# Three of four sine classes computed on ScalarE, products re-ordered and small transfers queued behind x's first tile, in a Fourier mixing + squared-ReLU kernel

## The chip, the cores and the metric

The kernel runs on one core of a Trainium2 chip. The metric is device time in microseconds (us) of one execution of the whole program. The times of the runs before the change lie between 1917.63 and 1918.9 us.

## The reference

```python
x        # (8, 3008, 256) float32
w_in     # (256, 2048), scaled by a float64 number, so float64
w_out    # (2048, 256), float64 in the same way

X = np.fft.fft(x, axis=1)            # along the sequence
X = np.fft.fft(X, axis=2).real       # along the features; keep the real part
h = X.reshape(24064, 256) @ w_in
g = np.maximum(h, 0) ** 2
out = (g @ w_out).astype(np.float32)
```

## The kernel before

**The mathematics.** The transform along the sequence is a product with cosine and sine tables. Rows of `x` are first folded: sums and differences of the rows n, S-n, M-n and M+n (S = 3008, M = S/2) halve the work several times, so that only S/4+1 row groups are left. The feature transform is folded into `w_in`: instead of transforming the features, the kernel multiplies `w_in` by a 256x128 cosine matrix (`cosd`, giving `G1`) and a sine matrix (`sind`, giving `G2`). The folded rows times cosine give `Pt`, times sine give `Qt`; both are 128 features by 1505 frequencies. A middle feature column is kept apart and handled by products called "E".

**The row tiles.** The row groups are cut into seven tiles, numbered 0 to 6. Tile 0 (95 rows) is the first class, tile 1 (94 rows) the second, tiles 2 and 3 (96 and 92 rows, `TWO` and `TWO + 1`) the third, and tiles 4, 5 and 6 (128, 128 and 120 rows, `ODD0` to `NT - 1`) the fourth. A product of a tile with its table has 95, 189 or 377 columns for each of two parities (`kp`). The tables `cosT` and `sinT` lie in SBUF, each tile's columns beside the next's. `load_table` fetches a tile's part in one to three transfers, since the rows that a tile needs are scattered in the array in device memory.

**Names for the steps.** In the hand-written order, "Pt" for a number t (P0, P1, ...) is the cosine product of tile t, "Qt" (Q0, Q1, ...) its sine product, and "Et" (E0, E1, ...) the cosine product of the lone middle column. Each is two matmuls on TensorE, one for each parity. `folds_of("P0")` is VectorE's work before the product P0, `folds_of("Q0")` that before Q0. `win[0][1]()` multiplies the first piece of `w_in` by `cosd` and `sind` (line 315) and copies the results to `G1` and `G2` on ScalarE (line 316). `p_part("copy")` is a pair of ScalarE copies of partial results (line 650, into `da`). The joins `join_4`, `join_2` and `lo` (lines 667 to 679, through `both`) combine the partial results on VectorE; `lo` writes `Pt` or `Qt`. `f_e` (line 518) is a tiny ScalarE operation that puts a tile's lone column into `lone` (shown as `wsum` in the profile) and must come before that tile's E product. `rounded` and `begin_win` change a piece of float64 weights into float32: VectorE lines 274, 276, 291, 293, 300, ScalarE lines 280, 281, 283.

**The order.** Nothing is re-ordered by a scheduler (`manual_schedule`): each engine executes its instructions in the order in which the program emits them, and a waiting instruction holds everything behind it on its engine. The code after `start()` (line 1062) is the first phase, the transform of batch element 0, which nothing precedes. It ends with `Qt` (line 667), the small product at line 828, and the first product of the main loop (lines 858 and 859). The main loop then runs over 8 batch elements x 6 frequency blocks x 8 pairs of feed-forward chunks; each step makes h (`front`), squares its positive part on ScalarE (`combine`) and multiplies by `w_out` (`back`). The transform of the next batch element is woven into it.

**The queues of the first phase.** SyncE (the SP queue) issues, in this order: x tiles 0 and 1, the first piece of `w_in` (two transfers), x tiles 2 and 3, `cosd`, `sind`, x tiles 4, 5, 6, cosine tables of tiles 4, 5, 6, sine tables of tiles 4, 5, 6, the next pieces of `w_in`. GpSimd (the POOL queue) issues: six transfers of the cosine tables of tiles 0 and 1, one of `alt_d` (a column of +1 and -1 that becomes the last column of `sind`), four of the cosine tables of tiles 2 and 3, ten of the sine tables of tiles 0 to 3. Each queue uses eight completion semaphores in turn: a transfer is issued only when the one eight places before it has landed.

**Keeping TensorE warm.** `awake(48)` at the start issues 48 products that nobody reads (tile `filled`, line 228); `awake(10)` does so again before the main loop.

Of the kernel before, what the change touches and what calls it, by code (L numbers as in the profile page):

```python
# [8 lines left out]
F32 = mybir.dt.float32  # L9
# [4 lines left out]
P = 128  # L14
# [23 lines left out]
def row_tiles(S):  # L38

    q = S // 4  # L40
    tiles, at = [], 0
    for count in (q // 2 + 1, q // 2):
        assert 2 * P < count <= 3 * P
        for r in range(0, count, P):
            tiles.append((at + r, min(P, count - r)))
        at += count
    return tiles


def class_tiles(S):  # L50


    half = S // 8 + 1
    tiles = []
    for c, order in enumerate((range(0, half, 4), range(2, half, 4), range(1, half, 2), range(half, S // 4 + 1))):
        size = -(-len(order) // -(-len(order) // P) // R) * R
        for r in range(0, len(order), size):
            tiles.append((c, order[r], order.step, len(order[r:r + size])))
    return tiles


def column_counts(S):

    counts = []
    for kp in range(2):
        n0 = len(range(kp, S // 4 + 1, 2))
        n1 = (n0 + 1) // 2
        n2 = (n1 + 1) // 2
        counts.append((n2, n2, n1, n0))
    return counts  # L70


def table_places(S):

    places, at = [], 0
    for c, *_ in class_tiles(S):
        places.append(at)
        at += column_counts(S)[0][c]
    return places, at
# [3 lines left out]
def kernel(  # L83
# [12 lines left out]
    nc = tc.nc  # L96
# [8 lines left out]
    CH = 256  # L105
    CK = 251
    NX = 3
    TILES = class_tiles(S)
    NT = len(TILES)
    NC = column_counts(S)  # L110
    PLACE, WT = table_places(S)
# [14 lines left out]
    psh = ctx.enter_context(tc.tile_pool(name="psh", bufs=2, space=PSUM))  # L126
    psd = ctx.enter_context(tc.tile_pool(name="psd", bufs=2, space=PSUM))
    psm = ctx.enter_context(tc.tile_pool(name="psm", bufs=1, space=PSUM))
# [5 lines left out]
    xt = {}  # L134
# [3 lines left out]
    ODD0 = NT - 3  # L138
# [15 lines left out]
    def later_rows(t):  # L154

        if t >= ODD0:
            return [(p, S // 8 + 1 + first, count, 1) for p, first, count in ODD[t - ODD0]]
        c, r0, step, rows = TILES[t]
        if t == TWO + 1:
            return [(p, TILES[TWO][1] + step * (2 * HALF2 - p - R), R, step) for p in range(0, ROWS2, R)]  # L160
        return [(0, r0, rows, step)]

    def load_x(b, t):
        if b and (t >= ODD0 or t == TWO + 1):
            xt[b, t] = xp.tile([P, 4, D], F32, name="xt", tag="x")
            for p, first, count, step in later_rows(t):
                nc.sync.dma_start(out=xt[b, t][p:p + count], in_=x[b, first:first + step * (count - 1) + 1:step])
            return
        c, r0, step, rows = TILES[t]

        while rows % 15 and rows % 16 and r0 + step * rows < NROW:
            rows += 1

        pool, tag = (gp, "g") if b == 0 and t < NT - NX else (xp, "x")
        xt[b, t] = pool.tile([P, 4, D], F32, name="xt", tag=tag)
        nc.sync.dma_start(out=xt[b, t][0:rows], in_=x[b, r0:r0 + step * (rows - 1) + 1:step])
# [8 lines left out]
    sind = const.tile([P, 2, P], F32, name="sind")  # L185
    cosT = const.tile([P, 2, WT], F32, name="cosT")
    sinT = const.tile([P, 2, WT], F32, name="sinT")
# [7 lines left out]
    def load_table(tab, src, tiles, queue=nc.sync):  # L195

        for t in tiles:
            c, r0, step, rows = TILES[t]
            for i, (s0, count) in enumerate(row_tiles(S)):
                mine = [r for r in range(count) if (s0 + r - r0) % step == 0 and 0 <= (s0 + r - r0) // step < rows]  # L200
                if mine:
                    o, m = (s0 + mine[0] - r0) // step, len(mine)
                    while m % 15 and m % 16 and o + m < P and mine[0] + step * m < P:
                        m += 1
                    nk = NC[0][c]
                    queue.dma_start(out=tab[o:o + m, :, PLACE[t]:PLACE[t] + nk],
                                    in_=src[mine[0]:mine[0] + step * (m - 1) + 1:step, :, i, 0:nk])

    make_identity(nc, ident)
    last = ident[:, P - 1:]  # L210

# [13 lines left out]
    def awake(n):  # L225
        filled = psh.tile([P, CH], F32, name="filled", tag="h")
        for _ in range(n):
            nc.tensor.matmul(filled[:, 0:P], ident, ident, start=True, stop=True)


    def pair_in(j):

        return moe_w_in.rearrange("(c p) (h j f) -> j c p h f", p=P, j=NJ, h=2)[j]
# [5 lines left out]
    def parts(w, k):  # L239
        return w.rearrange("p c (e h) -> p h (c e)", h=k)  # L240
# [10 lines left out]
    def load(src):  # L251

        nonlocal raws
        pool, tag = (gp, "g") if raws in (1, 2) else (xp, "x") if raws % (NX + 1) else (ep, "c")
        raws += 1
        single = src.dtype == F32
        raw = pool.tile([P, 2, CH, 1 if single else 2], src.dtype if single else U32, name="raw", tag=tag)
        for c in range(2):
            nc.sync.dma_start(out=raw[:, c].rearrange("p (o e) w -> p o (e w)", o=src.shape[2]),
                              in_=src[c] if single else src[c].bitcast(U32))  # L260
        return raw
# [44 lines left out]
    def begin_win(j, shared=False):  # L306

        w = ep.tile([P, 2, CH], F32, name="win", tag="sB" if j % 2 else "sA")
        finish = convert(parts(w, 1), win.pop(j, None) or load(pair_in(j)), shared)

        def products():
            for tab, G, nm in ((cosd, G1, "mC"), (sind, G2, "mD")):
                pg = psm.tile([P, CH], F32, name="pg", tag=nm)
                for i in range(2):
                    nc.tensor.matmul(pg, tab[:, i], w[:, i], start=i == 0, stop=i == 1)  # L315
                nc.scalar.copy(G.rearrange("p (h j f) -> j p h f", h=2, j=NJ)[j],
                               pg.rearrange("p (h f) -> p h f", h=2))

        def for_e():

            ps = psd.tile([P, CH], F32, name="pe", tag="d")
            for h in range(2):
                fc = j + NJ * h
                nc.tensor.matmul(ps[:, h:h + 1], G2[:, fc * P:(fc + 1) * P], last, start=True, stop=True)

            return lambda: nc.vector.tensor_scalar_mul(gE[:, j::NJ], ps[:, 0:2], 0.5)

        win[j] = finish, products, for_e
# [24 lines left out]
    turn = const.tile([P, 3, 4], F32, name="turn")  # L353
# [684 lines left out]
    def p_part(*names):  # L1038
        for nm in names:
            for kp in range(2):  # L1040
                groups[0, kp, nm]()
# [6 lines left out]
    def rounded(j):  # L1048
        halves, product, _ = win[j][0]
        halves()  # L1050
        product()


    def folds_of(names):
        for nm in names.split():
            (for_p if nm[0] == "P" else for_q)(int(nm[1:]))

    def products_of(names):
        for nm in names.split():
            (p_part if nm[0] == "P" else q_part)({"P": "", "Q": "", "E": "e"}[nm[0]] + nm[1:])  # L1060

    start()
    awake(48)
    load_x(0, 0)
    load_x(0, 1)
    nc.scalar.copy(turn[0:1, 0, 0:1], ident[0:1, 0:1])
    load_table(cosT, cos_s, (0, 1), nc.gpsimd)
    folds_of("P0 Q0 P1 Q1")
    begin_win(0)
# [2 lines left out]
    for dst, src, queue in ((cosd, cos_d, nc.sync), (sind[:, :, 0:P - 1], sin_d, nc.sync), (sind[:, :, P - 1:], alt_d, nc.gpsimd)):  # L1072
        queue.dma_start(out=dst, in_=src.rearrange("(c p) m -> p c m", p=P))
    load_table(cosT, cos_s, (TWO, TWO + 1), nc.gpsimd)
    for t in range(ODD0, NT):
        load_x(0, t)
    load_table(cosT, cos_s, range(ODD0, NT))
    load_table(sinT, sin_s, range(ODD0), nc.gpsimd)
    load_table(sinT, sin_s, range(ODD0, NT))
    win[1] = load(pair_in(1))  # L1080
    win[2] = load(pair_in(2))
    folds_of("P2")
    rounded(0)
    products_of("P0 P1")
    win[0][1]()
    products_of("E0 E1")
    folds_of("P3")
    products_of("P2 P3")
    p_part("copy")
    products_of("E2 E3")  # L1090
    folds_of("P4 P5 Q2 P6 Q3 Q4")
    products_of("P4 P5 P6 E4 E5 E6 Q0 Q1 Q2 Q3")
    for nm in ("join_4", "join_2", "lo"):
        groups[0, 0, nm]()
    folds_of("Q5")
# [101 lines left out]
    for i in range(len(steps) + LAG + 4):  # L1197
        if i < len(steps):
            b, k0, n, j = steps[i]
# [22 lines left out]
        if i >= LAG and flight:  # L1222
            at, g_, s_ = flight.pop(0)
# [75 lines left out]
```

## Time and profile before

| What | Value |
|---|---|
| Median of 3 runs | 1918.27 us (1917.63 to 1918.9) |
| The profiled execution: its time | 1918.66 us |
| The profiled execution: its span | 1916.9 us, with 1.8 us around it |
| TensorE (PE) busy, share of the span | 1906.6 us, 99% |
| VectorE (DVE) busy | 1443.3 us, 75% |
| ScalarE (ACT) busy | 954.7 us, 50% |
| GpSimd (POOL) busy | 1135.0 us, 59% |
| Granted TensorE clock, mean | 0.999 |
| Moved by DMA | 69.58 MB; of it 10.48 MB in the first 50 us |

The busy shares are averages over the whole span. The change touches only the first 40 us, where they are different, so this part has to be read from views that are cut by time: the busy time by stretches, the timeline, the waits, and the landing of transfers. In the timeline a line gives the start, the time from the first to the last of a group, the engine, the line of the kernel, what is written and read, how many, and in brackets how long the engine was idle before it and what ended that. A float32 product on TensorE shows as two records, so a count of 8 is four matmuls.

### The profile page before, as it was taken

The numbers are of one execution on the slowest core, as the hardware profiler recorded it, in microseconds if no ns is written. First come the engines' busy times: TensorE is split into PE (matmuls) and PEld (weight loads), VectorE is DVE, ScalarE is ACT, GpSimd is POOL, SyncE is SP. The second block draws the span as 40 slices with busy tenths as digits, with TensorE's granted clock in tenths as the row PEclk, the third lists the DMA queues.
The fourth block names the chain that finished last, engine by engine and source line by source line (L and its number), as shares of the span: only waits on it lengthen the run. The fifth ranks groups of instructions, "written<-read, shape, count | busy, mean of one in ns | idle before, by whom it ended". The sixth has DMA issues, their size and how long they took to land.

```text
span 1916.9 us, 28146 instructions
## 1 busy us (share of the span) xinstructions
PE 1906.6 (99%) x9250; PEld 1698.0 (89%) x9250; DVE 1443.3 (75%) x3645; ACT 954.7 (50%) x1207; POOL 1135.0 (59%) x1731
## 2 busy tenths in 40 slices
PE   9999999999999999999999999999999999999998
PEld 7888898888988898888988889888898888988887
DVE  8998887787678876787768877788767777655554
ACT  3755554555454544455444454455544555444444
POOL 3265655665566555655566665566655665566565
PEclk9999999999999999999999999999999999999999
DMA  8341211110111101111011100111001101100100
GB/s 219 116 46 28 56 28 37 28 45 13 28 36 42 34 12 36 33 42 28 12 36 47 36 20 12 47 39 34 23 20 44 36 12 22 28 12 12 22 12 23
DMA packets 145324, 69.58 MB, mean 36 GB/s; under 512 B 129176, under 2 KB 135786, under 8 KB 145176
## 3 DMA queue, kind: packets, MB, share of 16 engines
q1 hardware_dynamic: 144068, 66.40, 14.0%
q8 instruction: 73, 1.20, 0.3%
q0 software_dynamic: 832, 1.12, 0.3%
q14 instruction: 75, 0.61, 0.1%
q10 hardware_dynamic: 276, 0.26, 0.0%
HBM read 43.03 MB, written 24.69 MB: 35 GB/s over the span
## 4 chain that ended last, share of the span: by engine, by line
PE 96%; DVE 1%; DMA 1%; ACT 0%; issue 0%; SPq 0%; POOL 0%; DVEq 0%; ACTq 0%
PE ph L858 17%; PE ph L859 17%; PE mC L911 16%; PE mA L911 16%; PE mB L911 16%; PE mD L911 8%; PE pd L749 1%; PE pd L632 1%; PE mA L898 1%; DMA cosT<-in_cos_s_dram 1%; PE mB L898 1%; PE pd L723 1%; DMA xt<-in_x_dram 0%; PE pg L315 0%; DVE he L861 0%
## 5 line engine op out<-in xcount | busy, mean ns | idle before, releaser
L873 ACT ACTIVATE g<-g 128x1004 f32<-128x1004 f32 (+1 forms) x384 | 399.0, 1039 | 691.2 <-DVE g L864 445.4
L861 DVE SCALAR_TENSOR_TENSOR he<-Et,gE,ph 128x251 f32<-128x251 f32 (+1 forms) x768 | 362.6, 472 | 343.3 <-PE ph L859 338.0
L881 POOL TENSOR_TENSOR s<-g 128x251 f32<-128x251 f32 (+1 forms) x376 | 236.7, 630 | 637.1 <-ACT g L874 584.0
L858 PE MATMUL ph<-Pt,G 128*128 128x251 f32 (+1 forms) x1536 | 452.6, 376 | 0.4 <-DVE g L864 0.3
L859 PE MATMUL ph<-Qt,G 127*128 127x251 f32 (+1 forms) x1536 | 451.3, 374 | 0.0
L874 ACT ACTIVATE g<-g 128x1004 f32<-128x1004 f32 (+1 forms) x384 | 399.3, 1040 | 12.2
L911 PE MATMUL mC<-s,wsum 128*128 128x251 f32 (+1 forms) x1504 | 381.4, 375 | 0.0
L911 PE MATMUL mA<-g,wout 128*128 128x251 f32 (+1 forms) x1504 | 380.1, 374 | 0.0
L863 DVE TENSOR_TENSOR g<-he,ph 128x251 f32<-128x251 f32 (+1 forms) x768 | 320.5, 417 | 53.2 <-POOL s L881 1.4
L859 PEld LDWEIGHTS ph<-Qt,G 127*128 127x128 f32 x1536 | 291.5, 190 | 35.5
L858 PEld LDWEIGHTS ph<-Pt,G 128*128 128x128 f32 x1536 | 285.7, 189 | 34.4 <-DVE g L864 0.8
L911 PEld LDWEIGHTS mC<-s,wsum 128*128 128x128 f32 x1504 | 285.7, 190 | 34.4
L864 DVE TENSOR_TENSOR g<-he,ph 128x251 f32<-128x251 f32 (+1 forms) x768 | 314.3, 409 | 0.0
L911 PEld LDWEIGHTS mA<-g,wout 128*128 128x128 f32 x1504 | 282.7, 189 | 35.1 <-issue 0.3
L882 POOL TENSOR_TENSOR s<-s,g 128x251 f32<-128x251 f32 (+1 forms) x376 | 270.8, 720 | 29.5
L883 POOL TENSOR_TENSOR s<-g 128x251 f32<-128x251 f32 (+1 forms) x376 | 272.4, 724 | 0.0
L884 POOL TENSOR_TENSOR s<-g,s 128x251 f32<-128x251 f32 (+1 forms) x376 | 241.9, 643 | 0.0
L911 PE MATMUL mB<-g,wsum 128*128 128x251 f32 (+1 forms) x752 | 220.5, 374 | 0.0
L911 PE MATMUL mD<-s,wout 128*128 128x251 f32 (+1 forms) x752 | 220.4, 374 | 0.0
L911 PE MATMUL mB<-s,wout 128*128 128x251 f32 (+1 forms) x752 | 220.0, 374 | 0.0
L911 PEld LDWEIGHTS mB<-g,wsum 128*128 128x128 f32 x752 | 142.6, 190 | 17.3
L911 PEld LDWEIGHTS mD<-s,wout 128*128 128x128 f32 x752 | 142.0, 189 | 17.6
(182 smaller groups left out, 1398.7 us busy)
## 6 DMA issues: line engine op xcount, KB each, us to landing
out_dram<-os SPq DMA_DIRECT2D x376, 56.0 KB
xt<-in_x_dram SPq DMA_DIRECT2D x39, 384.0 KB
xt<-in_x_dram SPq DMA_DIRECT2D x63, 128.0 KB
Et<-e_dram SPq DMA_DIRECT2D x7, 752.5 KB
out_dram<-os SPq DMA_DIRECT2D x288, 6.8 KB
raw<-in_moe_w_in_dram SPq DMA_DIRECT2D x16, 256.0 KB
raw<-in_moe_w_out_dram SPq DMA_DIRECT2D x16, 256.0 KB
xt<-in_x_dram SPq DMA_DIRECT2D x2, 512.0 KB
```

The source lines that it names most:

```text
L858: nc.tensor.matmul(hP, G1[:, fs], pt[:, ks], start=True, stop=True)
L859: nc.tensor.matmul(hQ, G2[0:P - 1, fs], qt[0:P - 1, ks], start=True, stop=True)
L861: nc.vector.scalar_tensor_tensor(out=t, in0=et[:, ks], scalar=gE[:, fc:fc + 1], in1=hP, op0=ALU.mult, op1=ALU.add)
L863: tt(out=g[:, h, 0, 0:n], in0=t, in1=hQ, op=ALU.add)
L864: tt(out=g[:, h, 1, 0:n][:, ::-1], in0=t, in1=hQ, op=ALU.subtract)
L873: act(v, v, AF.Relu)
L874: act(v, v, AF.Square)
L881: gt(out=s1, in0=g21, in1=g22, op=ALU.add)
L882: gt(out=s2, in0=s1, in1=g11, op=ALU.subtract)
L883: gt(out=s3, in0=g11, in1=g21, op=ALU.subtract)
L884: gt(out=s4, in0=g12, in1=s2, op=ALU.subtract)
L911: nc.tensor.matmul(acc[nm][:, i, 0:n], w, v[:, 0:n], start=j == 0 and i == 0, stop=j == NJ - 1, skip_group_check=True)
```

## The change

Five things are changed, all in the first phase.

1. The sine tables of tiles 1 to 6 are no longer loaded. A new function `turn_table` makes each from the cosine table of the same tile: ScalarE reads the cosine columns in reverse order and multiplies every row by the +1 or -1 of `alt_d`. It is two ScalarE operations for a tile. The sine table of tile 0 is still loaded, in three transfers, by GpSimd, as before.
2. GpSimd copies one element of x's tile 0 into a spare place before it issues its first table transfer.
3. SyncE's order of x tiles and cosine tables from tile 4 on becomes: x 4, x 5, cosine 4, x 6, cosine 5, cosine 6.
4. The order of the products on TensorE is changed: each E product follows soon after its P product, Q0 and Q1 come before P4, and Q2 and Q3 come before E6. The products of the first piece of `w_in` come after E0 and E1, and for this piece use another PSUM buffer.
5. `awake(48)` becomes `awake(44)`.

VectorE's instructions and their order stay as they are. On TensorE the first phase has the same matmuls in another order, less four of `awake`:

```
before: P0 P1 | w_in | E0 E1 | P2 P3 | E2 E3 | P4 P5 P6 | E4 E5 E6 | Q0 Q1 Q2 Q3 | Q4 Q5 | Q6
after:  P0 P1 | E0 E1 | w_in | P2 E2 P3 E3 | Q0 Q1 | P4 E4 P5 E5 P6 | Q2 Q3 | E6 | Q4 Q5 | Q6
```

```diff
+    def turn_table(t):
+        c, at, rows = TILES[t][0], PLACE[t], TILES[t][3]
+        for kp in range(2):
+            nk = NC[kp][c]
+            nc.scalar.mul(sinT[0:rows, kp, at:at + nk], cosT[0:rows, kp, at:at + nk][:, ::-1], sind[0:rows, 0, P - 1:])
...
-                pg = psm.tile([P, CH], F32, name="pg", tag=nm)
+                pg = psm.tile([P, CH], F32, name="pg", tag=nm) if j else psh.tile([P, CH], F32, name="pg", tag="h")
...
-    awake(48)
+    awake(44)
     load_x(0, 0)
     load_x(0, 1)
     nc.scalar.copy(turn[0:1, 0, 0:1], ident[0:1, 0:1])
+    nc.gpsimd.tensor_copy(turn[0:1, 0, 1:2], xt[0, 0][0:1, 0, 0:1])
     load_table(cosT, cos_s, (0, 1), nc.gpsimd)
...
     load_table(cosT, cos_s, (TWO, TWO + 1), nc.gpsimd)
-    for t in range(ODD0, NT):
-        load_x(0, t)
-    load_table(cosT, cos_s, range(ODD0, NT))
-    load_table(sinT, sin_s, range(ODD0), nc.gpsimd)
-    load_table(sinT, sin_s, range(ODD0, NT))
+    load_table(sinT, sin_s, (0,), nc.gpsimd)
+    load_x(0, ODD0)
+    load_x(0, ODD0 + 1)
+    load_table(cosT, cos_s, (ODD0,))
+    load_x(0, ODD0 + 2)
+    load_table(cosT, cos_s, (ODD0 + 1, ODD0 + 2))
     win[1] = load(pair_in(1))
     win[2] = load(pair_in(2))
     folds_of("P2")
     rounded(0)
-    products_of("P0 P1")
+    products_of("P0 P1 E0 E1")
     win[0][1]()
-    products_of("E0 E1")
     folds_of("P3")
-    products_of("P2 P3")
+    products_of("P2 E2 P3 E3")
     p_part("copy")
-    products_of("E2 E3")
+    for t in range(1, ODD0):
+        turn_table(t)
+    products_of("Q0 Q1")
     folds_of("P4 P5 Q2 P6 Q3 Q4")
-    products_of("P4 P5 P6 E4 E5 E6 Q0 Q1 Q2 Q3")
+    for t in range(ODD0, NT):
+        turn_table(t)
+    products_of("P4 E4 P5 E5 P6 Q2 Q3 E6")
```

## The prediction

> **What bounds the kernel now.** I read the busy time by stretches first, because the change touches 40 us of 1917.
>
> ```profile
> 20.00:30.00 10.00, 8.74 (x32) 5.63 (x33) 9.48 (x28) 1.35 (x6) 1.95 (x4) 1.00 1.09 254
> 30.00:40.00 10.00, 10.00 (x57) 7.83 (x57) 8.55 (x26) 2.81 (x6) 1.28 (x1) 1.00 0.88 294
> 60.00:100.00 40.00, 40.00 (x197) 35.71 (x196) 36.70 (x86) 30.44 (x44) 9.54 (x7) 1.00 0.39 115
> ```
>
> The columns are stretch, length, then busy us of PE, weight loads, DVE, ACT, POOL, the granted clock, the DMA share and GB/s. From 60 us on PE is full, and the instructions there stay as they are: a delay or a gain of the first phase is passed on unchanged. Before 40 us PE, DVE and DMA are all nearly full, so the average does not tell which one is last. The timeline, DVE's lines first:
>
> ```profile
> 5.02 0.69 DVE L485 TENSOR_TENSOR fs<-xt 95x512 f32<-95x512 f32 x1 [3.44 <-DMA xt<-in_x_dram]
> ...
> 27.95 0.55 DVE L673 TENSOR_TENSOR Pt<-dc,pd 128x377 f32<-128x377 f32 x1
> ...
> 32.88 0.43 DVE L274 TENSOR_SCALAR fd<-raw 128x512 uint32<-128x512 uint32 x1 [1.18 <-DMA raw<-in_moe_w_in_dram]
> ...
> 38.77 1.12 DVE L667 SCALAR_TENSOR_TENSOR Qt<-pd,signs,w 128x377 f32<-128x377 f32 x2
> ```
>
> DVE starts when x's tile 0 has landed (5.02) and then works without a gap until 31.7, waits once, 1.18 us for the second piece of `w_in`, and goes on without a gap to the end of `Qt` at 39.9. So **VectorE's chain sets the end of the phase**, and the change leaves its instructions and order alone. It can gain only what DVE waits for. Now PE:
>
> ```profile
> 14.45 1.03 PE L632 MATMUL pd<-cosT,w 95*128 95x95 f32 x8
> ...
> 20.44 0.88 PE L632 MATMUL pd<-cosT,w 92*128 92x189 f32 x4 [0.59 <-DVE w L515]
> ...
> 26.26 1.50 PE L632 MATMUL pd<-cosT,w 120*128 120x377 f32 x4 [0.50 <-DMA cosT<-in_cos_s_dram]
> ...
> 27.60 3.96 PE L632 MATMUL pd<-cosT,wsum 128*128 128x377 f32 x12
> ...
> 31.39 4.86 PE L632 MATMUL pd<-sinT,w 95*127 95x95 f32 x24
> ```
>
> P6 (26.26) waits for the last cosine table; its first parity is done at about 27.1, before DVE's `lo` join (27.95) needs it. E4 to E6 and Q0 to Q5 follow densely behind P6. PE ends Q6 at 38.0, 0.8 us before `Qt`. Last, the small transfers on POOL:
>
> ```profile
> 3.08 3.48 POOL L206 DMA_DIRECT2D cosT<-in_cos_s_dram x6
> ...
> 11.26 2.38 POOL L206 DMA_DIRECT2D cosT<-in_cos_s_dram x3 [3.36 <-DMA cosT<-in_cos_s_dram]
> ```
>
> They are issued from 3.08 on, eight at once; the ninth waits for the first to land. The tile view of `cosT` gives 6.9/7.7/8.3 us (least, median, most) from issue to landing.
>
> **What the Trainium skill says.** "DMA: Bandwidth & Descriptors", section "Issuing engines are not separate DMA queues": transfers of all queues run on the same 16 engines and interleave. The trace agrees: small POOL transfers need 7.7 us beside SP's stream, while the 2.9 KB one issued at 40.19, when that stream has stopped, needs 1.6. "ScalarE: Activation LUTs", section "What ACT_TABLE_LOAD costs", prices an ACTIVATE at 186 ns + 0.833 ns an element, and 93 ns more for each per-partition operand. Line 280 (512 elements, one such operand) should cost 0.71 us and takes 0.72. "TensorE: Matmul & The Clock Gate", Part 1, puts the clock at half after an idle window of about 3.4 us. The trace shows the warming only: `filled` records are 0.213 us apart at the start and 0.112 later.
>
> **The change part by part.**
>
> *Tables not loaded.* SP loses three transfers (377, 377, 353 KB), POOL seven (348 KB); at the 254 GB/s of the stretch this is 5.7 us of transfer. On SP they stand before the second piece of `w_in`, which lands at 32.78 now. Of its 1.18 us wait nothing stays: **-1.2 us**. That is the whole gain on DVE. The new SP order puts x 6 behind cosine 4 (377 KB, 1.4 us): x 6 landed at 20.96 by the trace's landing events, will land near 22.2, and is needed at 22.05. I cost it at nothing, since the wait below comes later on DVE and takes it in; without that cover it is 0.2.
>
> *ScalarE's tables.* By the price above 0.27 to 0.36 us for an operation of 95 columns, 0.43 for 189, 0.59 for 377 (93 ns is saved back to back). Tiles 1 to 3: 2.1 us. Tiles 4 to 6: 3.2. ACT is busy 1.35 us in 20 to 30, so there is room, but ACT is in order: the `f_e` of tiles 4 and 5, which E4 and E5 need, stand behind the tables of tiles 1 to 3, and those behind the `da` copies, which wait for P3. Reading columns backwards is not in the trace; from no extra to double the price, 0 to 5 us on ACT. I take none, as no row suggests one; double would hold E4 by up to 2 us.
>
> *Small transfers behind x 0.* POOL's copy waits until x 0 has landed (4.99), so the first issue moves from 3.08 to about 5.2: 2.2 us later, and everything behind it on POOL with it. SP is not moved. Could x 0 land earlier? The first small packet starts at 7.76, after x 0 is in, so at most the 0.6 us by which one slow engine ends after the others. It would move the whole line and not the comparison; 0 to -0.6, I take 0. Now, with the latencies of before: cosine 0 and 1 land at 14.8 and 15.7 (12.7, 13.6 before). The first lands at 13.1 and frees the ninth: cosine 2 lands at 20.4 (18.55), cosine 3 at 22.1 (20.3), and sine 0, which must wait for cosine 1's semaphores, is issued at 15.5 to 16.7 and lands at about **24.3** (latencies 7.0 to 8.3: 23.7 to 25.0).
>
> *Products.* P0 and P1 can't start before 14.8 and 15.7, so the four `awake` products taken out (0.9 us) gain nothing. E0, E1 and the `w_in` products end at 18.4. P2 begins at 20.4, E2 follows, P3 at 22.1, E3 ends at 23.4. Then PE stands at Q0 for sine 0 until 24.3, **with P4 and all the rest queued behind it**. From the rows, a small matmul pair is 0.45 us (8 records 0.111 apart for two), a 377-column pair 1.27 (0.317 a record). Q0 Q1 end at 25.2. P4 E4 P5 E5 take 4 x 1.27 = 5.1, P6's first parity 0.63 and its end 0.16: 31.1. Cosine 5 and 6 (24.1 and 26.1 before) are in by then. So DVE's `lo` join moves from 27.95 to about 31.1: **+3.2 us**, a new DVE wait on PE. Three parts make it: Q0 Q1 ahead of P4 0.9, E4 E5 ahead of P6 2.5 (of which 1.3 goes into gaps: P4 starts at 22.44 and P6 at 26.26, 3.8 us for 2.5 of work), and late small tables 1.9 (Q0 at 24.3, where P4 starts at 22.44 now), less the 0.9 us that P6's first parity has in hand.
>
> *After that.* Behind P6 PE has Q2 Q3 1.3, E6 1.3, Q4 Q5 2.5, 0.4 and Q6 1.3 us: it ends at 38.5, and DVE comes to `Qt` at 38.77 + 2.0. So the earlier E products give nothing back at the end: PE's end was not last. Everything behind, DVE's work on weights and the first `he` (41.58), moves with it. The other PSUM buffer for `w_in` costs nothing: ScalarE empties it near 18.6, six us before P4 takes the place.
>
> **Sum:** +3.2 - 1.2 = +2.0 us on the profiled execution: 1918.66 + 2.0 = 1920.7. That execution is 0.39 above the median of the runs, so the median becomes **1920.3 us**. About 0.2% (3.8 us) is what a measurement of this kernel can tell from no change; +2.0 is within it.
>
> **Rivals.**
>
> *Slower by more than 0.2%: sine 0 holds PE still longer.* The mechanism is the wait at Q0. Each us by which sine 0 lands after 23.4 is a us of the end. It decides from a DVE wait of 5.0 us (5.0 - 1.2 = 3.8), which is P6's first parity at 32.95, so Q0 at 26.2: a latency of 9.5 us in place of 7.6. For it: SP now has bigger transfers outstanding while these are queued, and PE, with only about 60% work from 13.5 to 24, may drop to half its clock, which would add 2 to 3 us to the same chain. Against it: no latency in the trace is over 8.4 us, and gaps of 0.9 us left the clock full. It would give about 1918.3 + 4.7 = 1923.
>
> *No new wait.* If the small transfers need 4 to 5 us only, since fewer are queued, P2 and P3 run as before and Q0 doesn't wait: P6's first parity is done at 22.43 + 0.9 + 5.9 = 29.2, a DVE wait of 1.3: 1918.3 + 0.1. At best nothing is late and the 1.2 us is all gain: 1917.1, with an earlier x 0 1916.5. Against it: the 7.7 us held from 3 us to 22 us, in streams of different kind.
>
> *The change doesn't do what it says:* bytes are saved but DMA is not what DVE waits for, but for the 1.2 us. This I take as shown, and it is in the sum. A gain over 0.2% would need something that no row shows.
>
> **How the numbers follow.** The likeliest case, +0.8 to +3.6, has 0.46; slower by more than 0.2% 0.38; no new wait 0.12; an unseen gain 0.04. So faster 0.04, same 0.46 + 0.12 = 0.58, slower 0.38. The range reaches from 1917.3 (nearly the whole 1.2 gained) to 1924.3 (six us late: a sine 0 late by 2 us and a slow stretch of PE); the likeliest case alone is 1919.1 to 1921.9.
>
> **What would show it.** Right: in the profile after, DVE's first `Pt` join waits 2 to 4 us on PE; PE waits before its first `sinT` product for a POOL transfer; the 1.18 us wait on the second `w_in` piece is gone; the first small transfer is issued near 5.2; `he` starts near 43.6. Wrong: no wait at `Pt`, small transfers that land within 5 us, or an ACT table operation of over 0.8 us that holds E4.

## The result, and the profile after

The median of 20 runs is 1923.14 us (1918.64 to 1927.07), beside 1918.58 us for the kernel before, measured with it (1917.22 to 1923.34): a ratio of 1.0021, 95% interval 1.0014 to 1.0028. The forecast was 1920.3 us in a range of 1917.3 to 1924.3, with most of the chance on a difference within 0.2%. So the median is in the range, but outside the likeliest case of the forecast, +0.8 to +3.6 us: it is 4.6 us later.

The spread grew more than the median. Eight of the 20 runs lie between 1918.6 and 1921.4 us with a mean granted clock of 0.999 or 1.000. Twelve lie between 1922.2 and 1927.1 us with 0.998 or 0.997. The means of the two groups are 1920.0 and 1924.4 us. Of the 49 runs of the kernel before that stand beside the first experiments, four have 0.998. The profiled execution of the changed kernel, 1919.49 us with a span of 1917.7 (before: 1918.66 and 1916.9), is one of the first group, so this profile shows less than a fifth of what the median shows.

Busy time by stretches in this execution, columns as before:

```profile
20.00:30.00 10.00, 9.96 (x44) 6.91 (x43) 7.73 (x23) 5.67 (x18) 0.00 (x0) 1.00 0.87 248
30.00:40.00 10.00, 9.11 (x49) 6.87 (x47) 9.65 (x27) 3.09 (x7) 1.29 (x1) 1.00 0.36 118
60.00:100.00 40.00, 40.00 (x197) 35.71 (x196) 36.70 (x85) 30.66 (x44) 9.32 (x7) 1.00 0.39 117
```

From 20 to 30 us ScalarE is busy for 5.67 us where it was for 1.35, and VectorE for 7.73 where it was for 9.48: it now waits there. From 30 to 40 the DMA share falls from 0.88 to 0.36, since the tables are no longer loaded. From 60 us on TensorE is full, as before. The timeline (lines of the changed kernel are 8 higher than before):

```profile
4.60 0.69 DVE L493 TENSOR_TENSOR fs<-xt 95x512 f32<-95x512 f32 x1 [3.02 <-DMA xt<-in_x_dram]
...
5.27 3.51 POOL L206 DMA_DIRECT2D cosT<-in_cos_s_dram  x6
...
19.47 0.91 PE L640 MATMUL pd<-cosT,w 96*128 96x189 f32 x4 [1.53 <-DMA cosT<-in_cos_s_dram]
...
22.12 2.01 ACT L215 ACTIVATE sinT<-cosT,sind 94x95 f32<-94x95 f32 x6
...
22.56 1.09 PE L640 MATMUL pd<-sinT,w 95*127 95x95 f32 x8
...
23.49 1.46 PE L640 MATMUL pd<-cosT,w 128*128 128x377 f32 x4
...
24.32 3.09 ACT L215 ACTIVATE sinT<-cosT,sind 128x377 f32<-128x377 f32 x6
...
28.58 1.43 PE L640 MATMUL pd<-cosT,w 120*128 120x377 f32 x4
29.42 0.55 DVE L681 TENSOR_TENSOR Pt<-dc,pd 128x377 f32<-128x377 f32 x1 [1.96 <-PE pd L640]
...
33.09 0.42 DVE L282 TENSOR_SCALAR fd<-raw 128x512 uint32<-128x512 uint32 x1
...
38.98 1.12 DVE L675 SCALAR_TENSOR_TENSOR Qt<-pd,signs,w 128x377 f32<-128x377 f32 x2
...
40.16 0.69 PE L836 MATMUL pe<-Qt,ident 128*128 128x251 f32 x2 [1.05 <-DVE Qt L675]
...
41.79 0.48 DVE L869 SCALAR_TENSOR_TENSOR he<-Et,gE,ph 128x251 f32<-128x251 f32 x1 [0.95 <-ACT Et L837]
```

The small transfers are issued at 5.27, after x's tile 0. TensorE stands for 1.53 us at P2 (19.47) for a small cosine table, takes Q0 at 22.56 without a wait for its sine table, P4 at 23.49, and reaches P6 at 28.58. VectorE waits 1.96 us for P6 at the first `Pt` join (29.42), and no longer for the second piece of `w_in` (33.09). The first `he` is at 41.79, where it was at 41.58, and a product near the end of the main loop is later by the same 0.2 us (1862.84 and 1862.62). The other 0.6 us of the difference in span are at the very end: from the start of the last product to the end are 5.15 us, where they were 4.53.

### The profile page after: what moved, and what is told of

The parts are those of the page before. It is cut to its first block, busy times and chain, and to the rows that moved or that the text cites. A ratio compares the mean times of both kernels' runs of the same rounds, so it can differ in the third digit from the quotient of the medians.

```text
span 1917.7 us, 28135 instructions
## 1 busy us (share of the span) xinstructions
PE 1905.8 (99%) x9242; PEld 1696.6 (88%) x9242; DVE 1444.0 (75%) x3645; ACT 959.5 (50%) x1219; POOL 1132.4 (59%) x1725
## 3 DMA queue, kind: packets, MB, share of 16 engines
q8 instruction: 72, 1.18, 0.3%
## 4 chain that ended last, share of the span: by engine, by line
PE 96%; DVE 2%; DMA 1%; ACT 0%; issue 0%; POOL 0%; DVEq 0%; ACTq 0%
PE ph L866 17%; PE ph L867 17%; PE mC L919 16%; PE mA L919 16%; PE mB L919 16%; PE mD L919 8%; PE pd L757 1%; PE pd L640 1%; DMA cosT<-in_cos_s_dram 1%; PE mA L906 1%; PE mB L906 1%; PE pd L731 1%; DMA xt<-in_x_dram 0%; PE pg L323 0%; DVE he L869 0%
```

## The experiments

Each time is a median with its range. Each ratio is of means, to the runs of the kernel before on the same chip, with its 95% interval; where the runs fall into two groups it differs from the quotient of the medians. The medians of the kernel before were 1918.82 us beside `after_again`, `fill`, `no_copy` and `old_order`, 1918.58 beside `early`, `early_fill`, `copy_only` and `before_again`, and 1918.59 beside the rest. A mean clock of 0.998 or less over a run is called low below.

| Kernel | us | Ratio (95%) | first `Pt`, us | first `he`, us | clock halved in the profile |
|---|---|---|---|---|---|
| after (result) | 1923.14 (1918.64 to 1927.07) | 1.0021 (1.0014 to 1.0028) | 29.42 | 41.79 | no |
| before (first profile) | 1918.58 | | 27.95 | 41.58 | no |
| `after_again` | 1922.77 (1919.52 to 1926.5) | 1.0022 (1.0012 to 1.0032) | 32.66 | 45.03 | 21.75 to 28.57 |
| `fill` | 1920.74 (1920.12 to 1925.11) | 1.0014 (1.0007 to 1.002) | 30.59 | 42.96 | no |
| `no_copy` | 1918.57 (1917.67 to 1926.23) | 1.0005 (0.9997 to 1.0013) | 28.36 | 40.73 | no |
| `old_order` | 1921.63 (1918.08 to 1925.62) | 1.0013 (1.0006 to 1.002) | 29.73 | 44.13 | 20.61 to 27.43 |
| `early` | 1918.15 (1917.44 to 1923.11) | 0.9999 (0.9991 to 1.0007) | 30.75 | 45.15 | 22.40 to 29.23 |
| `early_fill` | 1918.04 (1917.52 to 1920.7) | 0.9998 (0.999 to 1.0006) | 27.57 | 39.95 | no |
| `copy_only` | 1921.18 (1917.34 to 1924.28) | 1.0007 (1.0001 to 1.0014) | 29.67 | 44.07 | 20.58 to 27.41 |
| `before_again` | 1918.59 (1917.29 to 1920.03) | 0.9999 (0.9991 to 1.0008) | 27.61 | 41.51 | no |
| `tables_only` | 1918.06 (1917.61 to 1918.85) | 0.9997 (0.9988 to 1.0005) | 27.38 | 41.16 | no |
| `copy_fill` | 1918.94 (1918.28 to 1920.11) | 1.0000 (0.9992 to 1.0008) | 28.38 | 42.78 | no |
| `fill_q` | 1922.0 (1918.54 to 1923.04) | 1.001 (1.0001 to 1.0018) | 28.68 | 41.04 | no |
| `early_fill_tail` | 1917.63 (1917.15 to 1918.8) | 0.9993 (0.9985 to 1.0001) | 27.95 | 40.81 | no |

The theory after the result: the copy makes the small tables late, TensorE stands before P2, and in part of the runs its clock then falls to half; P4 to P6 run at half speed and `Pt` waits for them. The rival: the late sine table and the new order of products alone hold `Pt`.

**The changed kernel again** (`after_again`, no edit), to have a profile of the other kind of run.

> The changed kernel once more, unedited, to see more of its spread. Theory (clock): the profile above, of a run of 1919.5, puts the main loop's first operation only 0.2 us later than before, which cannot make a median 4.6 us later; most runs lose the rest because TensorE falls to half its clock once more in the first 55 us. Then the runs lie between 1918.5 and 1927, most near 1923 to 1925, and the later ones show a lower mean granted clock (0.998 or 0.997). Rival (late tables): the spread comes from the landing of the small tables, the clock stays as it is, and the late runs show 0.999 or more.

This execution took 1922.77 us. Busy time by stretches of it, columns as before (the sixth after the length is the granted clock):

```profile
15.00:22.00 7.00, 5.31 (x31) 4.50 (x31) 6.72 (x18) 1.08 (x4) 0.78 (x2) 0.98 1.07 262
22.00:29.00 7.00, 7.00 (x21) 5.09 (x21) 5.17 (x16) 5.44 (x17) 0.00 (x0) 0.53 0.87 237
29.00:36.00 7.00, 7.00 (x28) 4.71 (x27) 3.13 (x10) 0.47 (x1) 0.00 (x0) 1.00 0.27 89
```

The clock is 0.53 from 22 to 29 us and full before and after. In the trace's clock records it is half from 21.75 to 28.57, 6.83 us. Its timeline there:

```profile
19.27 0.91 PE L640 MATMUL pd<-cosT,w 96*128 96x189 f32 x4 [1.33 <-DMA cosT<-in_cos_s_dram]
...
23.27 1.85 PE L640 MATMUL pd<-sinT,w 95*127 95x95 f32 x8
...
24.92 2.77 PE L640 MATMUL pd<-cosT,w 128*128 128x377 f32 x4
...
32.66 0.55 DVE L681 TENSOR_TENSOR Pt<-dc,pd 128x377 f32<-128x377 f32 x1 [5.25 <-PE pd L640]
...
45.03 0.48 DVE L869 SCALAR_TENSOR_TENSOR he<-Et,gE,ph 128x251 f32<-128x251 f32 x1 [0.95 <-ACT Et L837]
```

The gap before P2 is about as long as in the first profile, and sine 0 is not waited for. But P4 takes 2.77 us in place of 1.46, and the wait at `Pt` is 5.25 in place of 1.96. So `he` is 3.24 us later than in the other execution of the same program, about half of 6.83 us, which is what a stretch at half clock loses. This is the second group of runs.

**The gap filled** (`fill`): seven products that nobody reads stand before P2.

```diff
     folds_of("P3")
+    awake(7)
     products_of("P2 E2 P3 E3")
```

> The changed kernel with seven products that nobody reads on TensorE in the 1.5 us gap before P2. Theory (clock): the gap, with the thin work around it, is what lets the clock fall; filled, every run is near 1919.2 (0.2 to 0.8 above the kernel before) and the spread shrinks to that of before. Rival (late tables): the median stays at 1922 to 1924. Rival (clock, but lost elsewhere, near 40 to 55 us or at the end): the median stays, too, with a low clock.

Against `after_again` the median fell by 2.0 us and the mean by 1.4 (1922.83 to 1921.47). The intervals of the two ratios overlap, so the clear sign is the clock: it is low in two of 21 runs, where it was low in 17 of the 29 runs of the changed kernel. The run stays 1.5 us above the 1919.2 that I expected, and 1.9 us above the kernel before: the fall of the clock is one part of the cost, and late tables with the new order, the rival, are another. The fastest runs did not become faster (1920.12 and 1919.52 are the least of the two). The timeline says why:

```profile
19.67 0.91 PE L640 MATMUL pd<-cosT,w 96*128 96x189 f32 x4 [0.19 <-DMA cosT<-in_cos_s_dram]
...
23.73 1.09 PE L640 MATMUL pd<-sinT,w 95*127 95x95 f32 x8 [0.98 <-DMA sinT<-in_sin_s_dram]
...
30.59 0.55 DVE L681 TENSOR_TENSOR Pt<-dc,pd 128x377 f32<-128x377 f32 x1 [3.20 <-PE pd L640]
```

The gap before P2 is 0.19 us. Sine 0 landed at 23.6 here, where it landed at 22.4 in the first profile, and TensorE stood 0.98 us for it at Q0. The wait at `Pt` is then 3.20 us at full clock: the forecast's mechanism at the forecast's size. The size is right partly by luck: Q0 starts 0.6 us earlier than forecast (24.3), and VectorE comes to the join about as much earlier, since x's first tile was there at 4.54 and not at 5.02.

**Without the copy** (`no_copy`), the rest of the change kept.

```diff
-    nc.gpsimd.tensor_copy(turn[0:1, 0, 1:2], xt[0, 0][0:1, 0, 0:1])
```

> The changed kernel without GpSimd's copy of x's first element: the small transfers are issued from 3.1 us on again. Small tables 2.2 us earlier, no gap of 1.5 us before P2, x tile 0 at 4.99 instead of 4.57. Theory (clock): no gap, so the median falls to 1919 to 1920. The wait of DVE's Pt join on TensorE shrinks from 2.0 to about 0.8 or less, so the profile has the main loop's first operation near 41.2. Late tables: also better, by 1 to 2 us, with the clock unchanged. If the gap is not the cause, the median stays near 1923.

The median is 1918.57 us, 4.2 less than `after_again`; nine of 13 runs are at 1919.1 or less. Of its timeline:

```profile
17.74 0.80 PE L640 MATMUL pd<-cosT,w 96*128 96x189 f32 x4
...
20.11 0.88 PE L640 MATMUL pd<-cosT,w 92*128 92x189 f32 x4 [0.93 <-DVE w L523]
...
28.36 0.55 DVE L681 TENSOR_TENSOR Pt<-dc,pd 128x377 f32<-128x377 f32 x1 [1.07 <-PE pd L640]
```

P2 does not wait. P3 does, for a cosine table that lands at 19.97; the VectorE operation named in the line had ended about 3 us before. The 1.07 us that stay at `Pt` I put down to the new order of products, with Q0, Q1, E4 and E5 ahead of P6: with another order, in `early_fill` below, they are gone. Three of the 13 runs still have a low clock, up to 1926.23 us; they were not profiled, so whether P3's gap made it fall is not shown. `he` is 0.85 us earlier than before, but from the last product's start to the end are 5.38 us instead of 4.53, so the span is the same 1916.9 us.

**The former order of products** (`old_order`), with the tables, the copy and the SyncE order of the change.

```diff
-    products_of("P0 P1 E0 E1")
+    products_of("P0 P1")
     win[0][1]()
+    products_of("E0 E1")
...
-    products_of("P2 E2 P3 E3")
+    products_of("P2 P3")
     p_part("copy")
+    products_of("E2 E3")
...
-    products_of("Q0 Q1")
...
-    products_of("P4 E4 P5 E5 P6 Q2 Q3 E6")
+    products_of("P4 P5 P6 E4 E5 E6 Q0 Q1 Q2 Q3")
```

> The changed kernel with the products in their former order (E4 E5 E6 and Q0 to Q3 behind P6). My theory of the chain: P6 runs 3 us earlier, the Pt join has no wait on TensorE, the second piece of w_in is no longer waited for, x tile 0 lands 0.4 us earlier: the main loop's first operation near 40.0, 1.6 us earlier than before. Theory (clock): the gap before P2 is still there and becomes longer, as E2 is gone from behind it, so the spread stays: half of the runs at 1917, half 3 to 6 us later. Rival (the order of the products makes the spread): all runs near 1917.

It stayed late: 1921.63 us, with a low clock in 10 of 17 runs. Its profile has the clock at half from 20.61 to 27.43, after a gap of 1.33 us before P2; another of 0.80 before P3 began with the fall. The main loop near 40.0 that I expected at full clock is therefore not tested by this profile. That half of the runs would be at 1917 was wrong; the least is 1918.08. The median is 1.1 us below `after_again`, within the spread. The order of products is not what makes the late runs.

**The copy alone** (`copy_only`): the kernel before with this one line.

```diff
     nc.scalar.copy(turn[0:1, 0, 0:1], ident[0:1, 0:1])
+    nc.gpsimd.tensor_copy(turn[0:1, 0, 1:2], xt[0, 0][0:1, 0, 0:1])
```

> The kernel before, all its sine tables loaded and its order of products kept, with GpSimd's copy of x's first element alone added: the small transfers are issued 2.2 us later. Theory: the gap before P2 appears here too (cosine 2 lands near 20.5, in place of 18.6), with VectorE's chain having about 1 us in hand at Pt; the clock falls in a good part of the runs, and those are 2 to 5 us later; a run with full clock is at 1918.5 to 1919.5. Rival (the spread comes from the order of the products or from ScalarE's tables): all runs within 1 us of the kernel before.

The median rises by 2.6 us and the mean by 1.4, and 11 of 21 runs are above 1921 us, 10 of them with a low clock; of the 49 runs of the kernel before beside them, six are above 1921 us and four have a low clock, and of the 13 of `before_again` none. Busy time by stretches, cut at 3.4 us:

```profile
18.10:21.60 3.50, 2.09 (x11) 1.67 (x12) 3.36 (x11) 0.03 (x1) 1.37 (x3) 0.86 1.09 282
21.60:25.00 3.40, 3.40 (x12) 3.40 (x12) 3.26 (x9) 0.77 (x5) 1.60 (x3) 0.50 1.08 271
```

**The copy with the gaps filled** (`copy_fill`), which parts the late tables from the clock.

```diff
     folds_of("P3")
-    products_of("P2 P3")
+    awake(7)
+    products_of("P2")
+    awake(3)
+    products_of("P3")
```

> The kernel before with GpSimd's copy alone, as in an earlier run, and with products that nobody reads in the gaps that this opens: seven ahead of P2, three ahead of P3. Theory (the gap lets the clock fall): the clock stays, median 1918.5 to 1919.2, where the same kernel without the fill had 1921.2. Rival (late small tables delay by themselves): about 1921.

The same stretches of this kernel:

```profile
18.10:21.60 3.50, 3.17 (x26) 2.98 (x26) 3.35 (x10) 0.00 (x0) 0.78 (x2) 1.00 1.09 265
21.60:25.00 3.40, 2.54 (x17) 2.38 (x17) 3.26 (x10) 0.77 (x5) 2.18 (x4) 1.00 1.09 234
```

TensorE is busy for 3.17 us of the first stretch in place of 2.09, and the clock stays full. All 13 runs have 0.999 or more and end by 1920.11 us; the median is 1918.94. The transfers are the same, and the tables are no earlier than in `copy_only`: P2 starts at 20.58 and P3 at 23.01, where they started at 19.65 and 21.30. So the late tables alone cost 0.4 us in the median (0.2 in the mean), which is not clear of the noise; in the profiled execution, one of the latest of its runs, `he` is 1.2 us later than before. And the rest of the copy's cost, 2.2 us in the median (1.2 in the mean), goes with the clock. The intervals of the two ratios overlap; what is clear is the count, 10 low clocks of 21 without the products and none of 13 with them.

**P4, P5 and P6 first** (`early`), without the copy: the order that should need neither Q0 nor E4 ahead of `Pt`.

```diff
-    nc.gpsimd.tensor_copy(turn[0:1, 0, 1:2], xt[0, 0][0:1, 0, 0:1])
...
-    products_of("Q0 Q1")
...
-    products_of("P4 E4 P5 E5 P6 Q2 Q3 E6")
+    products_of("P4 P5 P6 Q0 Q1 E4 E5 E6 Q2 Q3")
```

> The changed kernel without GpSimd's copy, and with P4 P5 P6 ahead of everything that is not needed for the first Pt join (then Q0 Q1, E4 E5 E6, Q2 Q3); the sine tables still come from ScalarE. My theory: TensorE's half of the loss is gone, so VectorE's chain waits for nothing after x tile 0: no wait at Pt and none at the second w_in piece; main loop's first operation near 39.8 (41.58 less 1.2 less 0.6 for x tile 0), runs of full clock near 1917. One gap of about 1 us is left ahead of P3. Clock: if that is enough to let it fall, a part of the runs is 2 to 3 us later. Rival (the saved transfers bring nothing): near 41.5 and 1918.7 as before.

The median is 1918.15 us, the same as before within its interval; 11 of 13 runs are at 1919.5 or less. The profiled execution was the latest of its runs: the last small cosine table came late, P3 waited 3.50 us for it until 22.91, and the clock was at half from 22.40 to 29.23:

```profile
22.91 1.59 PE L640 MATMUL pd<-cosT,w 92*128 92x189 f32 x4 [3.50 <-DMA cosT<-in_cos_s_dram]
```

So this profile doesn't show the `he` near 39.8 that I expected at full clock; the next one does.

**The same with its gap filled** (`early_fill`).

```diff
-    products_of("P2 E2 P3 E3")
+    products_of("P2 E2")
+    awake(5)
+    products_of("P3 E3")
```

> As the run before it, with five products that nobody reads in the gap ahead of P3. Clock theory: no run has its clock fall in the first 45 us; median 1917.0 and a spread of no more than that of the kernel before. Rival (the clock falls for another reason, or the few products in the way cost more than they save): the same or a later median than without them.

Timeline:

```profile
18.55 1.28 PE L236 MATMUL filled<-ident 128*128 128x128 f32 x10
...
27.57 0.55 DVE L681 TENSOR_TENSOR Pt<-dc,pd 128x377 f32<-128x377 f32 x1
...
39.95 0.47 DVE L869 SCALAR_TENSOR_TENSOR he<-Et,gE,ph 128x251 f32<-128x251 f32 x1 [0.97 <-ACT Et L837]
```

`Pt` waits for nothing, and `he` is 1.63 us earlier than before, as expected. The time is 1917.86 us in this execution and 1918.04 in the median, where I expected 1917.0: half of the gain is lost again at the end of the program, where 5.29 us pass from the last product's start.

**The kernel before again** (`before_again`), to see how much x's first tile moves by itself.

> The kernel before, unedited, for a second profile. In the first one x tile 0 lands at 4.99, in five profiles of changed kernels at 4.4 to 4.6, one of them with the small transfers as early as here. If the landing of x tile 0 depends on none of the edits, it is at about 4.5 here too, and the main loop begins near 41.1; if something in the kernel before delays it, at 5.0. The time is 1918.7 either way.

VectorE first read its tile 0 at 4.66 us, where it was 5.02 in the first profile of the same program. So the 0.4 us by which the changed kernel starts earlier can't be put down to the change. `he` came only 0.07 us earlier, against 0.5 expected, because TensorE was then last: VectorE waited 1.44 us for the copy of a TensorE result.

**The tables alone** (`tables_only`): the kernel before with the sine tables of tiles 1 to 6 made on ScalarE, and nothing else.

```diff
...
+    load_table(sinT, sin_s, (0,), nc.gpsimd)
     for t in range(ODD0, NT):
         load_x(0, t)
     load_table(cosT, cos_s, range(ODD0, NT))
-    load_table(sinT, sin_s, range(ODD0), nc.gpsimd)
-    load_table(sinT, sin_s, range(ODD0, NT))
...
     products_of("E2 E3")
+    for t in range(1, ODD0):
+        turn_table(t)
     folds_of("P4 P5 Q2 P6 Q3 Q4")
+    for t in range(ODD0, NT):
+        turn_table(t)
```

> The kernel before with the sine tables of tiles 1 to 6 made by ScalarE, and no other edit: small transfers early, the former order of products and of SP's transfers, 48 products to keep TensorE warm. Theory: only the 1.2 us wait for the second w_in piece goes; TensorE has no new gap. Main loop's first operation near 40.3, 1.1 us earlier than before; the end of the program, which has been 0.6 us longer in the kernels with three SP transfers fewer, takes half of it back: median 1918.0, spread as before. Rival (the sine products now wait for ScalarE): no gain, the main loop at 41.5 or later.

The median is 1918.06 us, 0.5 less than before and within the interval. Timeline:

```profile
35.05 0.69 DVE L299 SCALAR_TENSOR_TENSOR fd<-raw,fd 128x512 uint32<-128x512 uint32 x1 [0.39 <-ACT fd L289]
...
37.40 2.39 PE L236 MATMUL filled<-ident 128*128 128x128 f32 x20
37.47 1.12 DVE L675 SCALAR_TENSOR_TENSOR Qt<-pd,signs,w 128x377 f32<-128x377 f32 x2
39.63 0.59 PE L836 MATMUL pe<-Qt,ident 128*128 128x251 f32 x2
...
41.16 0.48 DVE L869 SCALAR_TENSOR_TENSOR he<-Et,gE,ph 128x251 f32<-128x251 f32 x1 [1.83 <-ACT Et L837]
```

`Qt` starts 1.30 us earlier than before, but 0.64 of this is x's first tile (4.38 in place of 5.02). The wait of 1.18 us for `w_in` is gone, and 0.39 of it came back as a wait for ScalarE at line 299; so the saved loads gave VectorE about 0.7 us here. Then the product that reads `Qt` starts at 39.63, straight behind the 20 `filled` records and 1.0 us after `Qt`'s end. `he` gains 0.42 us only, where I expected 1.1. TensorE's end with these records, which I had left out, is next in line.

**Q0 and Q1 behind P6** (`fill_q`), on top of `fill`.

```diff
-    products_of("Q0 Q1")
...
-    products_of("P4 E4 P5 E5 P6 Q2 Q3 E6")
+    products_of("P4 E4 P5 E5 P6 Q0 Q1 Q2 Q3 E6")
```

> The changed kernel with the gap before P2 filled, as in an earlier run, and Q0 Q1 moved behind P6, so that TensorE doesn't stand at the sine table of tile 0 with P4 behind it. Theory: P4 follows E3 at once; against the run with the fill alone, the wait at Pt falls from 3.2 by 1.0 (the wait at Q0) and 0.9 (Q0 and Q1 themselves), to about 1.3; median 1920.7 less 1.9, that is 1918.8. Rival (P4 or P5 are held by their cosine tables anyway): less than 1 us gained.

In the profile the step is as large as expected: the wait at `Pt` is 1.49 us, and `he` 1.92 us earlier than in `fill`. Two things that I had not counted nearly cancel in it: the small cosine tables were there 0.5 us earlier, and E4 waited 0.43 us for its lone column, which stands behind the sine tables on ScalarE. The median is not as expected: 1922.0 us. Six of 13 runs are between 1918.5 and 1919.9, seven between 1922.0 and 1923.0, most of these with a clock of 0.999. The profiled execution is of the first kind, so what makes the second stays open.

**Three small transfers put back** (`early_fill_tail`): `early_fill` with three transfers of one column each on SyncE's queue in the main loop. The three sine tables that SyncE no longer loads had shifted, on all later transfers, which of the queue's completion semaphores each takes.

```diff
+    spare3 = const.tile([P, 3], F32, name="spare3")
...
+                for k in range(3):
+                    nc.sync.dma_start(out=spare3[:, k:k + 1], in_=alt_d[0:P])
```

> The best kernel so far (small transfers early, P4 P5 P6 first, gap filled: its main loop begins 1.6 us earlier than before, but its time is only 0.5 to 0.9 us shorter), with three transfers of 0.5 KB added on SP in the main loop, read by nobody, so that the number of SP's transfers is again that of the kernel before. In the profiles, the time from the last matmul to the end is 4.5 to 4.6 us in the kernels with the former number of SP transfers, and 5.0 to 5.4 with three fewer. Theory (the last transfers fall on other semaphores and places of the queue): back to 4.6, median about 1917.3. Rival (the end is longer for another reason): 5.2, median 1918.0.

From the last product's start to the end are 4.85 us, in place of 5.29; the median is 1917.63 us, 0.4 less than `early_fill`. Partly as expected: I had put 4.6 and 1917.3. `he` came 0.86 us later than in `early_fill` in this execution, so its own time, 1918.09, doesn't show the gain. In all profiles, the kernels with as many SyncE transfers as before have 4.53 to 4.85 us there, those with three fewer 4.96 to 5.38. So the number goes with the longer end in all 14 profiles. That it is the cause rests on this one pair, in which the end shrank by part of the difference, and by which way is not shown. This kernel is the best of all, 1 us below the one before, but the interval of its ratio still includes 1.

## Why the prediction was right or wrong

**In the range, but partly by luck.** The sum was +2.0 us. At `he` the profiled execution is only 0.2 later, and the median is at +4.6 mainly by two costs that the sum held at nothing: the clock and the end of the program. The errors have opposite signs, and that kept the result in the range.

**Right: the chain.** VectorE's chain did carry the change. The wait for `w_in` went, a wait for TensorE came at the first `Pt` join, behind P6, and a delay at `he` was handed through the main loop unchanged. Issue at 5.2 was 5.27. The small tables came later than before, and Q0 stood ahead of P4. But the sign that I had named, a wait before the first sine product, is in `fill` (0.98 us) and not in the profiled execution, where TensorE stood at P2 instead. ScalarE's tables took 2.01 and 3.09 us against 2.1 and 3.2, so the price that I worked out from the Trainium skill ("ScalarE: Activation LUTs", "What ACT_TABLE_LOAD costs") agrees with the trace, and reading backwards cost nothing extra.

**A size that was off: the latency of the small transfers.** I took 7.0 to 8.3 us from before. In the profiled execution it was 6.3 to 7.3, and they landed sooner than forecast: cosine 2 at 19.4 (forecast 20.4), cosine 3 at 20.9 (22.1), sine 0 at 22.4 (24.3). The forecast counted 1.9 us for late tables, as the distance from P4's former start, 22.44, to Q0; measured so it was 0.1. So in the profiled execution the new wait is 1.96 us where the term said 3.2. `he` is at 41.79, not 43.6: 1.2 us of that are the wait, and 0.4 that x's first tile was read at 4.60, a term that I took at 0 from a range of 0 to -0.6. In `fill` sine 0 landed at 23.6 and the wait was 3.20. The term was right in kind, and its size varies by over a microsecond between executions.

**A price given to the wrong case: the clock.** "May drop to half its clock, which would add 2 to 3 us" stood under the rival that ends slower, as a by-way of a late sine 0, and the argument against it was that gaps of 0.9 us had left the clock full. In the trace before, gaps between products were 0.59 us at most; 0.85 to 1.07 are gaps between weight loads. The gap before P2 became 1.53 us in the profiled execution and 1.33 in `after_again`. The clock falls in 12 of 20 runs if the mean clock is read so, and it adds 3.24 us in the pair of profiles. It should have been a case of its own, tied to thin work on TensorE around P2 and P3 and to no late sine table, and a likely one. The median run is one of those: as an estimate from the two profiles, 0.2 at `he`, 3.2 of clock and 0.6 at the end are 4.0 of its 4.6 us. The two groups of runs are 4.4 us apart in the mean, more than the 3.2 of the pair of profiles; the latest runs, with a clock of 0.997, were not profiled, and what they have beyond it stays open.

**A step that failed without harm: TensorE's end.** "PE's end was not last" took Q6's end, 38.0, and left out the 20 `filled` records behind it, which end with the start of the next product at 40.04, while `Qt` ended at 39.89. The two lines of the trace before:

```profile
37.81 2.39 PE L228 MATMUL filled<-ident 128*128 128x128 f32 x20
...
40.04 0.60 PE L828 MATMUL pe<-Qt,ident 128*128 128x251 f32 x2
```

So the 1.2 us were not "the whole gain on DVE" for the phase: alone the saved loads gave 0.42 at `he` (`tables_only`). The earlier E products do give something back there: Q6 starts at 35.37 in the changed kernel, 36.46 before. That is why VectorE's sum held for the changed kernel, where the product behind waits 1.05 us for `Qt`.

**Not foreseen: the end of the program.** 0.6 us are added where no instruction was edited.

**The rivals.** No new wait: refuted, the wait is in every profile of the changed kernel. That the change does not do what it says: alone, the saved loads were worth about 0.7 us to VectorE, 0.4 at `he`, and 0.5 in the median, which is not clear of the noise. Slower by more than 0.2%: with its mechanism refuted in part (Q0 does not stand until 26.2) and its clock branch right, it describes most runs. The ratio of the means lies 0.2% above 1, at the border.

## What to carry to other kernels

Before delaying a few transfers, ask which engine stands while they are late, and what the clock does when that engine thins out: here late tables by themselves cost little in the former order of products (0.4 us in the median of `copy_fill`), and the half clock cost 3.2 us in a pair of profiles of the changed kernel. It came in part of the runs, and a handful of unread products in the gaps left it in two of 21 runs (`fill`) or none of 13 (`copy_fill`). One profile can be of the kind of run that does not show this, so the spread and the mean clock of many runs are to be read beside it. In an in-order queue the join that is last should find its products first: P4, P5, P6 ahead of the rest took its wait away, and only then did the main loop start clearly earlier, by 1.6 us against both profiles of the kernel before (39.95 against 41.58 and 41.51).

## What the runs showed of the hardware

- The clock fell to half for 6.83 us in each of four profiles (`after_again`, `old_order`, `early`, `copy_only`) and came back by itself while TensorE was busy for 6.0 us or more of them. The Trainium skill, "TensorE: Matmul & The Clock Gate", Part 1, ties the fall in its table of states to an idle window of about 3.4 us, and tells further down of a kernel in which short idle times between groups of products made the clock swing. Only `early` had a gap as long (3.50 us), and the clock fell 3.0 us into it. The longest gaps ahead of the fall were 1.33 us in `after_again` and `old_order` and 0.67 in `copy_only`, and in the 3.4 us straight before the fall TensorE was busy for 2.12, 2.06 and 2.46 us. The measurement decides: a thin stretch is enough. The busy time alone does not tell which run falls, since the first profile of the changed kernel was busy for 1.88 us from 16.78 to 20.19 and kept its clock. Where the limit lies stays open.
- VectorE's first read of x's first tile, with the same transfers ahead of it, moved between 4.34 and 5.02 us over the profiles; in two of one program it was 5.02 and 4.66 (`before_again`).
- With three transfers fewer on SyncE's queue, the end of the program was 0.4 to 0.6 us longer (5.29 against 4.85 in the pair that differs in nothing else, 5.15 against 4.53 for the change). One pair alone parts the number of transfers from the other edits.
